# Joining the loads of a two-round decode kernel: 88 transfers for 101

## The chip, the core and the metric

The kernel runs on one core of a Trainium2 chip. A core has a matrix engine (PE, whose weight loads are listed as PEld), a vector engine (DVE), an activation engine (ACT), GpSimd (POOL), and a sequencer, SP, that here issues nearly all transfers from the chip's memory (HBM) to the on-chip SBUF. Sixteen DMA engines carry the transfers. The metric is the device time of one execution in microseconds (us); lower is better.

## What is computed

One decoding step for four sequences, `x` of 4 rows with 640 columns, in float32. A layer A (attention) and a layer B (an MLP) are applied alternately, twice, and both times with the same weights and the same caches:

```python
x = x + A(layernorm(x), k_cache, v_cache, wq, wo)
x = x + B(layernorm(x), w1, w2)
x = x + A(layernorm(x), k_cache, v_cache, wq, wo)
x = x + B(layernorm(x), w1, w2)
# A: 32 heads of 128; q = x @ wq; softmax(q k^T / sqrt(128)) v over the last 1024 cached positions; then @ wo
# B: relu(x @ w1) @ w2, with 1728 hidden columns
```

All of it rests on data that is used once in a round: 32 heads with their share of `wq`, 1024 keys and values for each of four sequences, and their share of `wo`, and then `w1` and `w2`.

## The kernel before

The host packs each head's data into one record of 9,472 float32 columns on 128 partitions (`REC`): 640 columns of `wq` (0 to `K`), 4,096 of keys (`K` to `V`), 4,096 of values (`V` to `WO`), and 640 of `wo`. A record is 4.85 MB. The 32 records lie one behind the other in HBM, so one transfer can span several records, or end inside one. `w1` and `w2` stand in a second array, `wm`.

SBUF holds five records at a time in a tile `store` (`NS = 5`), and beside it a tile `ring` of 4,832 columns and two tiles `kept` and `kept2` for parts that stay.

The kernel goes through two rounds. The first takes records 0 to 31 and then the MLP. The second begins with records 27 to 31, which are still in `store`, then takes 0 to 26, and then the MLP. For each record, PE computes the query (`query`, line 388), the scores of the keys (`scores`, 401), the weighted sum of the values (`values`, 438) and the product with `wo` (`project`, 457). The loop is skewed: in the step of record n, PE does the scores of n+1, the values of n, the query of n+2, and the projection of n, in this order. Every engine's instructions are in the order in which they are written.

Transfers are planned as a list, `items`, of source columns and a place in SBUF. The list is filled by small helpers: `piece` (207) loads columns of one record, `group` (211) loads several records in fewer transfers that are cut inside records, `ending` (217) orders the last three records of a round, and `weight` (197) loads columns of `wm`. `pump` (285) issues items in the order of the list, on SP's queue, and stops at the first one whose place still holds data in use. `done` (307) marks columns as used up after the instruction that reads them last, and calls `pump`. So a transfer is issued when the last column of its place has been read, and all later ones wait behind it.

`home(h, r)` (180) gives the place of record h: five places in turn. In the first round of the kernel before, record 0 comes in two transfers, records 1 to 4 in three (`FOUR`), record 5 in two, 6 to 9 in three, and 10 to 24 in three for each five (`FIVE`). The cut points of `FOUR` and `FIVE` lie inside records, so that the next transfer can start before the whole record has been read. Record 5 (`SIXTH`) keeps its last 2,176 columns in `kept2` for the second round, and record 26 its last 2,176 in `kept`.

At the change of rounds, record 0 is loaded into `ring` and into a free part of one place (`IN_RING`), while the MLP of the first round still empties `ring`; then the rest of record 0 and records 1 to 5 flow into the pieces of the five places as records 27 to 31 give them up. This is the list `places` (line 257), whose cuts fall where the engines' reads begin. After that, records have whole places again: 6, 7 and 8 one transfer each, 9 to 13 and 14 to 18 as `FIVE`, 19 to 23 as `LAST_FIVE`, and the last three by `ending`. The second MLP's weights go into two places of `store`.

The input `x` comes by four small transfers on ACT's queue at the start; PE's first matrix product waits for it. A wrapper class (line 94) issues all instructions, so most rows of the profile carry its line, L105 (L102 for the first of an engine); rows are told apart by their tiles. `misc<-xT,store` is a query, `sc_ps<-store,qT` scores, `o_ps<-store,scratch` values, `acc<-store,oTs` a projection, `sc_ps<-store,xT` the MLP's first product and `acc<-store,scratch` its second.

Of the kernel before, what the change touches and what calls it, by code (L numbers as in the profile page):

```python
# [32 lines left out]
F32 = mybir.dt.float32  # L33
# [5 lines left out]
P = 128  # L39
B, D, H, DH, W, FF = 4, 640, 32, 128, 1024, 1728  # L40
NB = 4
FD = D // NB
# [4 lines left out]
WQ, K, V, WO = 0, D, D + 4 * W, D + 8 * W  # L47
REC = 2 * D + 8 * W
HALF = REC // 2
VH = 2 * W  # L50

NS = 5
# [5 lines left out]
TCOLS = len(TILES) * FD  # L58
RING = 4832
KEPT = WO - 3 * 512  # L60
SIXTH = 5
KEPT2 = WO - 3 * 512
PARKED = 2048
FROM = V - 512
W2 = KB * FF
# [6 lines left out]
            (W2 + 2560, W2 + 4480, "spare", 0), (W2 + 4480, W2 + 6080, "ring", 0), (W2 + 6080, W2 + 7840, "ring", 1600),  # L72
            (W2 + 7840, WM, "ring", 3456)]

IN_RING = [(640, 1152, "ring", 4256), (1152, 3200, "spare", 0), (3200, 4736, "ring", 0), (4736, 6272, "ring", 1536),
           (6272, 7296, "ring", 3072), (8832, 8992, "ring", 4096)]
IN_SLOT = [(0, K), (7296, WO), (8992, REC)]

CUTS = [*range(0, K, DH), *range(K, WO, 512), *range(WO, REC + 1, FD)]
W1_SLOT = [[0, 1], [2], [3], [4]]  # L80
W2_SLOT = [22, 20, 8, 4]
LATE = 6

# [29 lines left out]
def decode_kernel(ctx: ExitStack, tc: tile.TileContext, xf, rec, wm, out):  # L113
    nc = tc.nc
    pe, dve, act, pool, sp = (InOrder(tc, e) for e in (nc.tensor, nc.vector, nc.scalar, nc.gpsimd, nc.sync))
    sb = ctx.enter_context(tc.tile_pool(name="sb", bufs=1))
# [72 lines left out]
    buffers = {"store": store, "ring": ring, "kept": kept, "kept2": kept2}  # L189

    def load(src, lo, hi, buf, col, parts):
        items.append((src[:, lo:hi], buf, col, hi - lo, parts))

    def place(buf, col):
        return ("store", spare * REC + FROM + col) if buf == "spare" else (buf, col)

    def weight(r, lo, hi, buf, col):
        buf, col = place(buf, col)
        load(wm, lo, hi, buf, col, [(("w", r), lo, hi, col)])


    def run(r, lo, hi, buf, col):
        parts = [(("rec", r, h), max(lo - h * REC, 0), min(hi - h * REC, REC), col + max(h * REC - lo, 0))
                 for h in range(lo // REC, (hi - 1) // REC + 1)]
        load(rec, lo, hi, buf, col, parts)

    def piece(r, h, lo, hi, buf="store", col=None):
        run(r, h * REC + lo, h * REC + hi, buf, home(h, r) * REC + lo if col is None else col)


    def group(r, h, sizes):
        lo = 0
        for size in sizes:
            run(r, h * REC + lo, h * REC + lo + size, "store", home(h, r) * REC + lo)
            lo += size

    def ending(r, hs, late):
        a, b, c = hs[-3:]
        end = WO if late else REC
        last = WO if late else KEPT  # L220
        for h, lo, hi in ((a, 0, V), (b, 0, V), (a, V, end), (c, 0, V), (b, V, end), (c, V, V + VH), (c, V + VH, last)):
            piece(r, h, lo, hi)
        if late:
            for h in hs[-1:] + hs[-LATE:-1]:
                if h == LAST - 1:
                    piece(r, h, WO, REC, "kept", WO - KEPT)
                else:
                    piece(r, h, WO, REC)


    hs = order[0]
    piece(0, hs[0], 0, V)
    piece(0, hs[0], V, REC)
    group(0, 1, FOUR)
    for h in hs[5:-3]:
        if h in GROUPS[0]:
            group(0, h, GROUPS[0][h])
        if any(g <= h < g + sum(z) // REC for g, z in GROUPS[0].items()):
            continue
        piece(0, h, 0, KEPT if h == LAST - 1 else KEPT2 if h == SIXTH else WO if h >= H - LATE else REC)  # L240
        if h == SIXTH:
            piece(0, h, KEPT2, REC, "kept2", 0)
# [18 lines left out]
    stream = [(new[0], lo, hi) for lo, hi in IN_SLOT] + [(h, 0, KEPT2 if h == SIXTH else REC) for h in new[1:6]]  # L261
    for buf, lo, hi in places:
        while stream:
            h, c, end = stream[0]
            cut = max(x for x in [*CUTS, end] if x <= min(end, c + hi - lo))
            if cut <= c:
                break
            piece(1, h, c, cut, buf, lo)
            lo += cut - c
            stream[:1] = [(h, cut, end)] if cut < end else []  # L270
    assert not stream
    for h in new[6:-3]:
        if h in GROUPS[1]:
            group(1, h, GROUPS[1][h])
        if not any(g <= h < g + sum(z) // REC for g, z in GROUPS[1].items()):
            piece(1, h, 0, REC)
    ending(1, hs, False)
    for ks in W1_SLOT:
        weight(1, ks[0] * FF, (ks[-1] + 1) * FF, "store", home(LAST + 1, 0) * REC + ks[0] * FF)
    n = 0  # L280
    for size in W2_SLOT:
        weight(1, W2 + n * FD, W2 + (n + size) * FD, "store", home(LAST + 2, 0) * REC + n * FD)
        n += size

    def pump():

        while items:
            src, buf, col, n, parts = items[0]
            if any(b == buf and x < col + n and col < y for b, x, y in live):
                return  # L290
            sp.dma_start(buffers[buf][:, col:col + n], src)
            live.append((buf, col, col + n))
            for key, lo, hi, c in parts:
                at.setdefault(key, []).append((lo, hi, buf, c))
            items.pop(0)
# [19 lines left out]
    def free(buf, a, b):  # L315
        if a < b:
            rest = []
            for bb, u, v in live:
                if bb != buf or v <= a or b <= u:
                    rest.append((bb, u, v))  # L320
                else:
                    rest += [(bb, p, q) for p, q in ((u, a), (b, v)) if p < q]
            live[:] = rest


    def park(i):
        a = spare * REC + FROM
        to, lo, hi = ((misc, 0, 512), (sc_ps[1], 512, 1536), (o_ps, 1536, 2048))[i]
        act.copy(to, store[:, a + lo:a + hi])
        free("store", a + lo, a + hi)  # L330
        pump()

    def unpark(i):
        b = home(LAST, 0) * REC
        a = b + (K, K + 512, K + VH, K + VH + 512)[i]
        copy = dve.tensor_copy if i in (1, 2) else act.copy
        copy(store[:, a:a + 512], (sc_ps[1][:, :512], sc_ps[1][:, 512:], o_ps, misc)[i])
        live.append(("store", a, a + 512))
        if i == 2:
            dve.memset(o_ps, 0.0)  # L340
        if i == 3:
            c = spare * REC
# [160 lines left out]
    for r in range(2):  # L503
        hs = order[r]
# [8 lines left out]
        if r:  # L513
            unpark(2)
            unpark(3)
        weights(0, ((0, 1), (1, 2)))
        for n, h in enumerate(hs[:-2]):
            i = n - (H - late)
# [3 lines left out]
            end = n == H - 3  # L522
# [17 lines left out]
        if not r:  # L540
            park(0)
# [5 lines left out]
        if not r:  # L547
            park(1)
        output_T(late - 2)
        if not r:  # L550
            park(2)
# [50 lines left out]
```

## Time and profile before

| | |
|---|---|
| three runs | 712.23, 712.61, 714.89 us; median 712.61 |
| the profiled execution | 711.53 us, its span 709.7 us |
| mean granted PE clock | 0.819 |
| busy: PE, DVE, ACT | 71%, 45%, 14% of the span |
| record and weight transfers (SP's queue q1) | 14,544 packets, 301.69 MB |
| mean rate over the span | 426 GB/s |

The span runs from the first to the last instruction; the time of a run holds a little more. Busy digits are tenths of a slice, of which the span has 40. A packet is what one DMA engine moves at a time: a transfer to 128 partitions has one for each partition's row of columns, eight on each engine, and one small packet for each engine that reports its end: 144 in all, and 101 transfers make 14,544. In the list of DMA issues, the last number is the time from issue to landing, which includes all the work that stands in the queue ahead.

### The profile page before, as it was taken

The page shows a single profiled execution, that of the slowest core. Times are in us where ns is not written, and L with a number is a line of the kernel's source. Part 1 is how long each engine was busy: PE and PEld are TensorE (multiplying, and loading weights), DVE is VectorE, ACT ScalarE, POOL GpSimd, SP SyncE. Part 2 cuts the span into 40 slices and gives each one's busy share as a digit, 9 for nine tenths or more (in the row PEclk, how much of TensorE's full clock was granted, in tenths as well). Part 3 has the DMA queues.
Part 4 walks back from the last instruction along what each step waited for, and adds up shares of the span by engine and source line. Part 5 has one row for each costly group of instructions (what it writes and reads, how often), then busy time and mean ns, then how long its engine had stood idle before and what let it go on. Part 6 is the DMA issues. An engine that isn't in the chain of part 4 may idle for free.

```text
span 709.7 us, 8716 instructions
## 1 busy us (share of the span) xinstructions
PE 503.7 (71%) x3722; PEld 203.4 (29%) x3722; DVE 317.4 (45%) x647; ACT 101.4 (14%) x216; POOL 1.1 (0%) x9
## 2 busy tenths in 40 slices
PE   4388386478566578879878898675577686776885
PEld 2123132232232223333313333231222231233322
DVE  3244253253443453545641866634244252453661
ACT  0111010011010110111120321201011011011120
POOL 0000000000000000000000000000000000000000
PEclk9987787577787776877999999968677676897899
DMA  9999999999999999999999999999999999999997
GB/s 400 421 453 408 454 410 459 417 439 441 428 433 426 424 451 420 424 425 430 427 408 408 417 435 422 448 425 453 428 428 437 439 432 430 432 427 419 427 425 303
DMA packets 14614, 302.24 MB, mean 426 GB/s; under 512 B 1632, under 2 KB 2032, under 8 KB 6256
## 3 DMA queue, kind: packets, MB, share of 16 engines
q1 hardware_dynamic: 14544, 301.69, 99.2%
q8 instruction: 29, 0.48, 0.2%
q14 instruction: 9, 0.07, 0.0%
q10 hardware_dynamic: 32, 0.01, 0.0%
HBM read 301.61 MB, written 0.08 MB: 425 GB/s over the span
## 4 chain that ended last, share of the span: by engine, by line
DMA 73%; PE 21%; DVE 3%; issue 1%; ACT 1%; another core or an unknown queue 0%; SPq 0%; ACTq 0%; DVEq 0%
DMA store<-rec 67%; PE o_ps L105 8%; PE sc_ps L105 7%; DMA store<-wm 3%; DMA ring<-wm 3%; PE misc L105 3%; PE acc L105 3%; DVE scratch L105 1%; DVE o_ps L105 1%; ACT oTs L105 1%; DVE small L105 0%; DVE store L105 0%; PE t_ps L105 0%; SPq L105 0%
## 5 line engine op out<-in xcount | busy, mean ns | idle before, releaser
L105 PE MATMUL sc_ps<-store,qT 128*4 128x512 f32 x1014 | 190.6, 837 | 24.4 <-DMA store<-rec 22.4
L105 PE MATMUL misc<-xT,store 128*128 128x4 f32 x620 | 97.2, 283 | 121.4 <-DMA store<-rec 121.1
L105 PE MATMUL o_ps<-store,scratch 128*16 128x512 f32 x954 | 143.8, 680 | 2.2 <-DMA store<-rec 1.2
L105 PEld LDWEIGHTS misc<-xT,store 128*128 128x128 f32 x620 | 91.8, 230 | 178.5 <-DMA store<-rec 145.7
L105 DVE TENSOR_REDUCE small<-sc_ps 128x1 f32<-128x1024 f32 x64 | 78.3, 1224 | 139.9 <-PE sc_ps L105 139.9
L105 ACT ACTIVATE sc_ps<-sc_ps,small 128x1024 f32<-128x1024 f32 (+1 forms) x68 | 71.1, 1046 | 319.6 <-DVE small L105 318.3
L105 DVE STREAM_TRANSPOSE sc_ps<-sc_ps 128x1024 f32<-128x1024 f32 (+1 forms) x70 | 81.7, 1167 | 0.1
L105 DVE TENSOR_TENSOR qT<-misc,rows 128x4 f32<-128x4 f32 x61 | 9.5, 155 | 135.6 <-PE misc L105 135.6
L105 DVE TENSOR_TENSOR o_ps<-o_ps,of_block 128x512 f32<-128x512 f32 x62 | 43.3, 699 | 52.3 <-PE o_ps L105 50.9
L105 PEld LDWEIGHTS o_ps<-store,scratch 128*16 128x16 f32 x954 | 33.3, 114 | 114.4 <-issue 101.1
L105 PEld LDWEIGHTS sc_ps<-store,qT 128*4 128x4 f32 x1014 | 32.5, 106 | 107.8 <-issue 65.4
L105 PE MATMUL acc<-store,oTs 128*4 128x160 f32 x478 | 34.3, 368 | 17.2 <-ACT oTs L105 16.4
L105 DVE TENSOR_REDUCE scratch<-o_ps 128x128 f32<-128x512 f32 x62 | 42.9, 691 | 2.1
L105 ACT COPY oTs<-o_ps 128x4 f32<-128x4 f32 x62 | 10.1, 162 | 226.6 <-PE o_ps L105 226.6
L105 PE MATMUL o_ps<-rows,scratch 128*128 128x4 f32 x124 | 27.0, 288 | 13.2 <-DVE scratch L105 13.0
L105 PEld LDWEIGHTS o_ps<-rows,scratch 128*128 128x128 f32 x124 | 22.8, 229 | 20.8 <-DVE scratch L105 17.7
L105 DVE TENSOR_TENSOR scratch<-sc_ps,mrt 128x128 f32<-128x128 f32 (+1 forms) x70 | 19.6, 280 | 2.7
L105 DVE TENSOR_SCALAR mrt<-of_batch,small 128x4 f32<-128x4 f32 x64 | 14.7, 229 | 2.2
L105 PE MATMUL acc<-kept,small 128*1 128x344 f32 (+1 forms) x44 | 14.7, 445 | 0.0
L105 PEld LDWEIGHTS acc<-store,oTs 128*4 128x4 f32 x478 | 6.6, 84 | 23.2 <-ACT oTs L105 21.2
L105 DVE STREAM_TRANSPOSE scratch<-small 128x32 f32<-128x32 f32 x64 | 12.8, 201 | 0.8 <-ACT sc_ps L105 0.8
L105 ACT ACTIVATION_READ_ACCUMULATOR sc_ps<-sc_ps,small 128x1 f32 x64 | 12.3, 193 | 0.0
(86 smaller groups left out, 118.1 us busy)
## 6 DMA issues: line engine op xcount, KB each, us to landing
store<-rec SPq DMA_DIRECT2D x10, 7872.0 KB, 28.9
store<-rec SPq DMA_DIRECT2D x5, 7936.0 KB, 33.4
store<-rec SPq DMA_DIRECT2D x14, 2368.0 KB, 27.3
store<-rec SPq DMA_DIRECT2D x6, 4736.0 KB, 26.7
store<-rec SPq DMA_DIRECT2D x4, 6336.0 KB, 27.7
store<-rec SPq DMA_DIRECT2D x2, 7104.0 KB, 29.7
store<-rec SPq DMA_DIRECT2D x2, 6272.0 KB, 43.6
store<-rec SPq DMA_DIRECT2D x2, 4416.0 KB
```

The source lines that it names most:

```text
L105: r = build(*args, **kwargs)
```

## The change

The first 2,176 columns of record 0 (the query weights and three blocks of keys; `FIRST = K + 3 * 512`) get a place of their own in front of the five places, and `store` grows by as much. `kept2` goes. Record 0 is loaded in the first round at column 0 of `store`, records 0 to 4 lie one behind the other from there, and all later records use the five places shifted by `FIRST`. So the first columns of record 0 are still there in the second round, and only columns 2,176 onward are loaded again. Record 5 is loaded whole in the second round.

Transfers are joined:

- in the first round, records 0 to 24 come five at a time in three transfers, from the very first record on;
- at the end of a round, the first of the last three records comes in one transfer and not two;
- at the change of rounds, record 0 takes four transfers and one for its `wo`, and records 1 to 5 flow as one stream whose transfers may cross from one record to the next (14 transfers); one place piece now spans two neighbouring places;
- in the second round, records 6 to 8 come in two transfers (`THREE`);
- two of the four `w1` pieces of the second MLP are joined.

The instructions of the computing engines stay as they are, apart from the columns that they read.

```diff
-SIXTH = 5
-KEPT2 = WO - 3 * 512
+FIRST = K + 3 * 512
...
-IN_RING = [(640, 1152, "ring", 4256), (1152, 3200, "spare", 0), (3200, 4736, "ring", 0), (4736, 6272, "ring", 1536),
-           (6272, 7296, "ring", 3072), (8832, 8992, "ring", 4096)]
-IN_SLOT = [(0, K), (7296, WO), (8992, REC)]
+IN_RING = [(2176, 2688, "ring", 4256), (2688, 4736, "spare", 0), (4736, 6272, "ring", 0), (6272, 8832, "ring", 1536)]
...
-W1_SLOT = [[0, 1], [2], [3], [4]]
+W1_SLOT = [[0, 1], [2, 3], [4]]
...
-FOUR = [REC + 3200, REC + 3072, 2 * REC - 6272]
 FIVE = [REC + 6272, 2 * REC - 3072, 2 * REC - 3200]
 LAST_FIVE = [REC + 4736, 2 * REC - 4736, REC, REC]
-GROUPS = [{6: FOUR, 10: FIVE, 15: FIVE, 20: FIVE}, {9: FIVE, 14: FIVE, 19: LAST_FIVE}]
+THREE = [REC + HALF, REC + HALF]
+GROUPS = [{h: FIVE for h in range(0, 25, 5)}, {6: THREE, 9: FIVE, 14: FIVE, 19: LAST_FIVE}]
...
-    store = sb.tile([P, NS * REC], F32, name="store")
+    store = sb.tile([P, FIRST + NS * REC], F32, name="store")
...
-    kept2 = sb.tile([P, REC - KEPT2], F32, name="kept2")
...
     def home(h, r):
 
-        return h % NS if not r or h >= LAST else (h - 6 + LAST) % NS
+        if r:
+            return FIRST + (h if h >= LAST else h - 6 + LAST) % NS * REC
+        return (0 if h < NS else FIRST) + h % NS * REC
...
-    at = {("rec", 1, LAST - 1): [(KEPT, REC, "kept", 0)], ("rec", 1, SIXTH): [(KEPT2, REC, "kept2", 0)]}
+    at = {("rec", 1, LAST - 1): [(KEPT, REC, "kept", 0)], ("rec", 1, 0): [(0, FIRST, "store", 0)]}
...
-        for h, lo, hi in ((a, 0, V), (b, 0, V), (a, V, end), (c, 0, V), (b, V, end), (c, V, V + VH), (c, V + VH, last)):
+        for h, lo, hi in ((a, 0, end), (b, 0, V), (c, 0, V), (b, V, end), (c, V, V + VH), (c, V + VH, last)):
...
-    piece(0, hs[0], 0, V)
-    piece(0, hs[0], V, REC)
-    group(0, 1, FOUR)
-    for h in hs[5:-3]:
+    for h in hs[:-3]:
         if h in GROUPS[0]:
             group(0, h, GROUPS[0][h])
...
-    places = [("store", old[i] * REC + lo, old[i] * REC + hi) for i, lo, hi in (
-        (0, 0, K), (0, K + 1024, K + VH), (0, K + VH + 1024, V), (1, 0, K + VH), (1, K + VH, V), (0, V, WO), (0, WO, REC),
-        (2, 0, V), (1, V, REC), (3, 0, V), (2, V, REC), (4, 0, FROM), (3, V, REC),
-        (4, FROM + PARKED, REC), (4, FROM, FROM + PARKED))] + [("ring", 0, RING)]
+    places = [("store", old[i] + lo, old[j] + hi) for i, lo, j, hi in (
+        (0, 0, 0, K), (0, K + 1024, 0, K + VH), (0, K + VH + 1024, 0, V), (1, 0, 1, K + VH), (1, K + VH, 1, V),
+        (0, V, 0, WO), (0, WO, 0, REC), (2, 0, 2, V), (1, V, 1, REC), (3, 0, 3, V), (2, V, 2, REC), (3, V, 4, FROM),
+        (4, FROM + PARKED, 4, REC), (4, FROM, 4, FROM + PARKED))] + [("ring", 0, RING)]
...
+    cuts = [h * REC + x for h in new[1:6] for x in CUTS]
+    c, end = new[1] * REC, new[6] * REC
     for buf, lo, hi in places:
...
+        if lo == old[0] + WO:
+            piece(1, new[0], WO, REC, buf, lo)
+        elif c < end:
+            cut = max(x for x in cuts if x <= min(end, c + hi - lo))
+            run(1, c, cut, buf, lo)
+            c = cut
```

More of the change, by code (lines that the diff above doesn't have):

```diff
@@ L180, in home @@
     def home(h, r):
-        return h % NS if not r or h >= LAST else (h - 6 + LAST) % NS
+        if r:
+            return FIRST + (h if h >= LAST else h - 6 + LAST) % NS * REC
+        return (0 if h < NS else FIRST) + h % NS * REC
     items = []
-    at = {("rec", 1, LAST - 1): [(KEPT, REC, "kept", 0)], ("rec", 1, SIXTH): [(KEPT2, REC, "kept2", 0)]}
+    at = {("rec", 1, LAST - 1): [(KEPT, REC, "kept", 0)], ("rec", 1, 0): [(0, FIRST, "store", 0)]}
     live = []
     spare = home(H - 1, 0)
-    buffers = {"store": store, "ring": ring, "kept": kept, "kept2": kept2}
+    buffers = {"store": store, "ring": ring, "kept": kept}
     def load(src, lo, hi, buf, col, parts):
@@ L194, in place @@
     def place(buf, col):
-        return ("store", spare * REC + FROM + col) if buf == "spare" else (buf, col)
+        return ("store", spare + FROM + col) if buf == "spare" else (buf, col)
     def weight(r, lo, hi, buf, col):
@@ L207, in piece @@
     def piece(r, h, lo, hi, buf="store", col=None):
-        run(r, h * REC + lo, h * REC + hi, buf, home(h, r) * REC + lo if col is None else col)
+        run(r, h * REC + lo, h * REC + hi, buf, home(h, r) + lo if col is None else col)
     def group(r, h, sizes):
@@ L213, in group @@
         for size in sizes:
-            run(r, h * REC + lo, h * REC + lo + size, "store", home(h, r) * REC + lo)
+            run(r, h * REC + lo, h * REC + lo + size, "store", home(h, r) + lo)
             lo += size
@@ L231, in decode_kernel @@
     hs = order[0]
-    piece(0, hs[0], 0, V)
-    piece(0, hs[0], V, REC)
-    group(0, 1, FOUR)
-    for h in hs[5:-3]:
+    for h in hs[:-3]:
         if h in GROUPS[0]:
             group(0, h, GROUPS[0][h])
[L238 to L242, printed above, removed]
+        if h >= 25:
+            piece(0, h, 0, KEPT if h == LAST - 1 else WO if h >= H - LATE else REC)
         if h == LAST - 1:
@@ L256, in decode_kernel @@
         piece(1, new[0], lo, hi, *place(buf, col))
-    places = [("store", old[i] * REC + lo, old[i] * REC + hi) for i, lo, hi in (
-        (0, 0, K), (0, K + 1024, K + VH), (0, K + VH + 1024, V), (1, 0, K + VH), (1, K + VH, V), (0, V, WO), (0, WO, REC),
-        (2, 0, V), (1, V, REC), (3, 0, V), (2, V, REC), (4, 0, FROM), (3, V, REC),
-        (4, FROM + PARKED, REC), (4, FROM, FROM + PARKED))] + [("ring", 0, RING)]
-    stream = [(new[0], lo, hi) for lo, hi in IN_SLOT] + [(h, 0, KEPT2 if h == SIXTH else REC) for h in new[1:6]]
-    for buf, lo, hi in places:
[L263 to L271, printed above, removed]
+    places = [("store", old[i] + lo, old[j] + hi) for i, lo, j, hi in (
[4 more added lines that the diff above has]
+    c, end = new[1] * REC, new[6] * REC
+    for buf, lo, hi in places:
+        if lo == old[0] + WO:
[4 more added lines that the diff above has]
+            c = cut
+    assert c == end
     for h in new[6:-3]:
@@ L278, in decode_kernel @@
     for ks in W1_SLOT:
-        weight(1, ks[0] * FF, (ks[-1] + 1) * FF, "store", home(LAST + 1, 0) * REC + ks[0] * FF)
+        weight(1, ks[0] * FF, (ks[-1] + 1) * FF, "store", home(LAST + 1, 0) + ks[0] * FF)
     n = 0
     for size in W2_SLOT:
-        weight(1, W2 + n * FD, W2 + (n + size) * FD, "store", home(LAST + 2, 0) * REC + n * FD)
+        weight(1, W2 + n * FD, W2 + (n + size) * FD, "store", home(LAST + 2, 0) + n * FD)
         n += size
@@ L326, in park @@
     def park(i):
-        a = spare * REC + FROM
+        a = spare + FROM
         to, lo, hi = ((misc, 0, 512), (sc_ps[1], 512, 1536), (o_ps, 1536, 2048))[i]
@@ L333, in unpark @@
     def unpark(i):
-        b = home(LAST, 0) * REC
+        b = home(LAST, 0)
         a = b + (K, K + 512, K + VH, K + VH + 512)[i]
@@ L341, in unpark @@
         if i == 3:
-            c = spare * REC
+            c = spare
             at["rec", 1, H - 1] = [(0, FROM, "store", c), (FROM, V, "store", a), (V, V + 1024, "store", b + K),
```

## The prediction

> **What bounds the kernel now.** I read the page first: busy shares, DMA queues, the chain that ended last and the DMA issues.
>
> ```profile
> span 709.7 us, 8716 instructions
> PE 503.7 (71%) x3722; PEld 203.4 (29%) x3722; DVE 317.4 (45%) x647; ACT 101.4 (14%) x216; POOL 1.1 (0%) x9
> DMA  9999999999999999999999999999999999999997
> q1 hardware_dynamic: 14544, 301.69, 99.2%
> DMA 73%; PE 21%; DVE 3%; issue 1%; ACT 1%; another core or an unknown queue 0%; SPq 0%; ACTq 0%; DVEq 0%
> store<-rec SPq DMA_DIRECT2D x10, 7872.0 KB, 28.9
> out<-scratch SPq DMA_DIRECT2D x1, 80.0 KB, 1.6
> ```
>
> The transfers that SP issues keep the 16 DMA engines at 99.2% of the span; no slice but the last is below 9. PE is busy 71%, but mostly waits for data and catches up. So the time is bytes over rate, plus what each transfer adds, plus a head and a tail. A wait of PE counts only if it lets the DMA queue run empty.
>
> Next the DMA view by stretch, first of long loads, then of mixed ones, then of short ones around the change of rounds:
>
> ```profile
> DMA packets 433, 24.23 MB, mean 433 GB/s; under 512 B 47, under 2 KB 47, under 8 KB 47
> ...
> DMA packets 1960, 25.59 MB, mean 427 GB/s; under 512 B 220, under 2 KB 220, under 8 KB 768
> ...
> DMA packets 1955, 8.07 MB, mean 404 GB/s; under 512 B 219, under 2 KB 475, under 8 KB 1664
> ```
>
> These are 134 to 190, 300 to 360 and 380 to 400 us. Each transfer leaves 16 packets under 512 B (one an engine), so the three stretches hold about 3, 14 and 14 transfers.
>
> **The change: the term that counts.** The bytes do not change: the second round skips 2,176 columns of the first record, where it skipped 2,176 columns of the sixth, and the SBUF reserved is the same. PE, DVE and ACT do the same work on the same shapes. So what goes is 13 transfers of 101: 5 in round one's records, 5 at the change of rounds, 2 in round two's records, 1 in the weights.
>
> Price of one: at 433 GB/s the 8.07 MB of the third stretch take 18.64 us; they took 20, so 1.36 us for 13.7 transfers, 0.10 us each. The 25.59 MB of the second take 59.10; they took 60, so 0.90 over 13.75, 0.065 each. I take the middle, 0.08, since the 13 lie in both kinds of stretch: 13 x 0.08 = 1.05 us. Ends: 0 (the skipped overheads may be refilled by skew between engines) and 13 x 0.10 = 1.4. SP also issues 13 times 0.33 us less, hidden, since SP mostly waits.
>
> [...]
>
> **What hides the joins.** A joined load is issued when the last of its places is free, so later. It costs nothing while the queue still has work. I call margin: time from issue to landing, less the load's own time at 433 GB/s, less 1.4 us of latency (the 80 KB store lands after 1.6 and moves for 0.2).
>
> (a) The first five records. Three loads of 7.9 MB replace five. The DMA view from 1.6 to 2 us has the first packets (there are none before 1.6), and then comes PE's start (columns: start, duration, work, idle before):
>
> ```profile
> DMA packets 9, 0.17 MB, mean 426 GB/s; under 512 B 0, under 2 KB 0, under 8 KB 0
> ...
> 9.64 0.87 PE L102 MATMUL acc<-scratch,ring 128*128 128x160 f32 x2 [9.64 <-DMA scratch<-xf]
> 11.79 2.29 PE L105 MATMUL misc<-xT,store 128*128 128x4 f32 x10 [0.27 <-DVE xT L105]
> 16.67 1.89 PE L105 MATMUL sc_ps<-store,qT 128*4 128x512 f32 x8
> 29.43 2.29 PE L105 MATMUL misc<-xT,store 128*128 128x4 f32 x10 [10.87 <-DMA store<-rec]
> 35.35 2.42 PE L105 MATMUL o_ps<-store,scratch 128*16 128x512 f32 x16
> ...
> q10 hardware_dynamic: 32, 0.01, 0.9%
> ...
> store<-rec SPq DMA_DIRECT2D x1, 2368.0 KB, 8.2
> ...
> 9.01 0.33 SPq L105 DMA_DIRECT2D store<-rec  x1
> ...
> store<-rec SPq DMA_DIRECT2D x1, 6336.0 KB, 51.6
> ```
>
> The first load (issued at 0.8) landed at 9.0, the fifth record at 9.01 + 51.6 = 60.6. The input x, on ACT's queue (q10), came at 9.64, just behind the first load: its 32 small packets all went between 4.5 and 9.2 us, taking turns with that load's rows. Now the first load is 8.06 MB, 18.6 us instead of 5.6, and rows are 3.3 times as long. x then comes some 0.6 x 3.3 = 2 us behind a landing at about 21.5: 23.5 (ends 21.5 and 1.8 + 7.8 x 3.3 = 27.6). PE starts 14 us later. From x to the end of the first scores takes 8.9 (9.64 to 18.56), the next query to the first values 8.3 (29.43 to 37.77), one more record 8.8 (504.02 to 512.81, rows below): the place of the next load is free at 23.5 + 26.0 = 49.5. The three loads end at about 60.4, so it had to be issued by 59. Margin 9.5 us: the late start is hidden.
>
> The second load of the next group needs more than in the old alignment, as the places sit 2,176 columns further on: values of the fourth record, not only the output of the third. That step in the trace (a load landing, 146.84 + 25.4 = 172.2, and PE after it):
>
> ```profile
> 146.84 0.33 SPq L105 DMA_DIRECT2D store<-rec  x1
> ...
> store<-rec SPq DMA_DIRECT2D x1, 7872.0 KB, 25.4
> ...
> 179.58 0.33 SPq L105 DMA_DIRECT2D store<-rec  x1
> ...
> 182.31 2.34 PE L105 MATMUL o_ps<-store,scratch 128*16 128x512 f32 x16
> ```
>
> Output after 7.3, first half of values after 182.31 + 1.2 - 172.2 = 11.3. So issue at 60.4 + 11.3 = 71.7, needed by 60.4 + 18.6 - 1.4 = 77.6: margin 5.9. The load issued at 146.84 lives with 25.4 - 18.6 - 1.4 = 5.4, and the queue stays full.
>
> (b) The change of rounds. The tightest issue:
>
> ```profile
> 394.33 0.33 SPq L105 DMA_DIRECT2D store<-rec  x1
> ...
> store<-rec SPq DMA_DIRECT2D x1, 1344.0 KB, 6.4
> ```
>
> Own time 3.2, so margin 6.4 - 3.2 - 1.4 = 1.8. Ahead of it the first record's rest is 160 columns (0.2 us) shorter, the next pieces 32 columns longer (0.04), and three transfers fewer stand there (0.25): 1.4 us left, tight but positive. The place is freed by a resident record's scores, which wait for no new load. The last ring load now waits for the MLP's last tiles, about 0.4 us later, under that same queue.
>
> (c) The sixth to eighth new record of round two come in two loads, and the group after them needs the fifth's values:
>
> ```profile
> 457.17 0.33 SPq L105 DMA_DIRECT2D store<-rec  x1
> ...
> store<-rec SPq DMA_DIRECT2D x1, 7872.0 KB, 46.8
> ...
> 504.02 2.29 PE L105 MATMUL misc<-xT,store 128*128 128x4 f32 x10 [11.34 <-DMA store<-rec]
> 510.92 1.89 PE L105 MATMUL o_ps<-store,scratch 128*16 128x512 f32 x16
> ```
>
> Landed at 504.0, so the loads before it end at 485.4 and the first of the two joined ones 16.8 earlier, at 468.6. PE then needs 8.1 (504.02 to the first half of values at 512.1): issue at 476.7 instead of 457.2, needed by 484. Margin 7.3.
>
> (d) The tail. Record 24 (first of the last three) lands whole, one 2.4 MB load (5.6 us) later:
>
> ```profile
> 646.61 0.33 SPq L105 DMA_DIRECT2D store<-rec  x1
> ...
> store<-rec SPq DMA_DIRECT2D x1, 2368.0 KB, 35.9
> ...
> 663.09 1.28 PE L105 MATMUL misc<-xT,store 128*128 128x4 f32 x10
> ...
> 695.99 0.91 PE L105 MATMUL sc_ps<-store,xT 128*4 128x432 f32 x8 [0.69 <-DMA store<-wm]
> 700.26 1.80 PE L105 MATMUL acc<-store,scratch 128*4 128x160 f32 x44 [2.38 <-DMA store<-wm]
> 703.96 1.27 PE L105 MATMUL acc<-store,scratch 128*4 128x160 f32 x32 [1.90 <-DMA store<-wm]
> ...
> 706.30 0.11 PEld L105 LDWEIGHTS acc<-store,scratch 128*4 128x4 f32 x8 [0.34 <-DMA store<-wm]
> ```
>
> The last of five such loads landed at 682.5, so the second at 682.5 - 3 x 5.6 = 665.7; less 1 us saved by then, 664.7. The query at 663.09 becomes 1.7 us late. PE's waits for weights at 695.99, 700.26 and 703.96 (0.7, 2.4, 1.9 us) absorb it even though the weights come 1 us sooner. The joined weight pieces land where the second did. No price.
>
> Sum: the profiled execution took 711.53 us (span 709.7); 711.53 - 1.05 = 710.5. The median of the three runs, 712.61, stands 1.1 above it; I forecast on the median: 712.61 - 1.05 = **711.5 us**.
>
> **Rivals.**
> 1. *x comes much later (slower).* If x's four small loads each wait for a whole load of SP's queue, x comes with the third load, at 60.4; the place for the fourth is free at 60.4 + 26.0 = 86.4, and the queue stands empty from 60.4 to 87.8: 712.6 + 27.4 - 1 = 739. Against it: 32 packets within 4.5 to 9.2 us, during one load. It costs from x at 33 on, and decides (over 0.5%) from 38. 3 in 100. [...]
> 2. *The turn runs dry (slower).* If the joined places come free a scores step (1.9 us) later at each of four joins, 7.6 us stand against the 1.4 of margin: 712.6 - 1 + 6.2 = 718. For it: the smallest margin. Against: the steps that free them are in the same order. Decides from 6 us late. 6 in 100.
> 3. *More gain (faster).* 301.69 MB at 433 GB/s is 696.7; with the 1.8 before the first packet and 3.4 after the last (706.30 to the span's end), 702. All transfers together lose 7.6; were all of that in the 13, 705. 4 in 100.
> 4. *Each transfer's latency is not hidden (faster):* 13 x 1.4 = 18, so 694. The DMA row of nines speaks against it; 3 in 100.
>
> **How the numbers follow.** The forecast has 84 in 100. Its range takes the term's ends (0 to 1.4) and the spread of the runs (711.5 to 714.9, the profiled one among them): 709.7 to 714.0. That leaves out the rivals, 16 in 100. A change within 0.5% (3.6 us, about what a measurement of this kernel can tell from none) is the forecast alone: faster 0.07, same 0.84, slower 0.09.
>
> **What would show it.** Right: q1 packets 14544 - 13 x 144 = 12,672 with 301.69 MB, DMA share still 99%, PE's first matmul at 22 to 28 us, an issue of a 7.9 MB load near 50 us, 404 GB/s risen around the turn. Wrong: any slice but the last under 9 in the DMA row, above all near 60, 79, 395 or 485 us; or a tail after the last load longer than 3.5 us.

## The result, and the profile after

| | before | after |
|---|---|---|
| median of the runs (22 each, on one chip) | 712.88 us | 715.06 us |
| lowest to highest | 711.47 to 714.89 | 712.60 to 717.20 |
| the profiled execution, its span | 711.53 us, 709.7 us | 715.46 us, 713.7 us |

The ratio after to before is 1.0027, with a 95% interval of 1.0018 to 1.0037: the change costs some 2 us. That is within the 0.5% which the prediction called no change, but it has the wrong sign, its interval excludes 1, and 715.06 us lies above the predicted range of 709.7 to 714.0. The ratios in this text are those on record for the runs, and not quotients of the two medians that stand beside them.

The page of the changed kernel, in the rows that answer to those shown of before (DMA share by slice, GB/s by slice, the queue of records and weights, and the chain that ended last):

```profile
DMA  9999999999999999999999999999999999999997
GB/s 396 448 404 449 441 415 441 444 419 435 440 431 424 447 427 424 416 447 421 423 382 376 381 435 427 454 430 436 440 422 435 440 426 430 440 422 430 427 425 293
...
q1 hardware_dynamic: 12672, 301.68, 98.8%
...
DMA 28%; PE 16%; DVE 4%; issue 1%; ACT 1%; DVEq 0%; ACTq 0%
```

The packets are the 12,672 that 88 transfers should leave, 144 each (in the trace of the changed kernel the store of the output, alone in its stretch from 710 us on, left 128 packets of 512 B to 2 KB and 16 under 512 B), and the bytes are the same. The row of nines hides the loss: a 9 is anything from 90% up, and the slices are 17.8 us long. The GB/s row below it shows it. Slices 21 to 23, from 357 to 410 us, move 382, 376 and 381 GB/s, and no other slice between the first and the last is that low.

The same stretch by windows (columns: window; length, then busy time and count of PE, PEld, DVE, ACT and POOL; granted PE clock; DMA share; GB/s), before:

```profile
360.00:400.00 40.00, 31.21 (x336) 12.44 (x328) 14.35 (x45) 9.10 (x18) 0.00 (x0) 1.00 1.02 407
364.00:372.00 8.00, 4.96 (x43) 1.40 (x41) 1.61 (x8) 1.19 (x2) 0.00 (x0) 1.00 1.01 403
...
380.00:400.00 20.00, 16.95 (x186) 7.96 (x184) 10.40 (x32) 5.53 (x10) 0.00 (x0) 1.00 1.02 404
```

and after:

```profile
360.00:400.00 40.00, 32.75 (x326) 12.30 (x330) 15.50 (x49) 10.36 (x20) 0.00 (x0) 0.92 0.96 369
364.00:372.00 8.00, 7.40 (x90) 2.91 (x82) 4.02 (x13) 3.31 (x6) 0.00 (x0) 1.00 0.89 340
...
380.00:400.00 20.00, 17.81 (x188) 7.75 (x184) 7.72 (x26) 4.32 (x8) 0.00 (x0) 0.84 0.96 353
```

In these 40 us the rate falls by 38 GB/s, so 1.52 MB less is moved. At the full queue's 433 GB/s (before, 134 to 190 us) that is 3.5 us, most of the 4.0 us by which the profiled spans differ. Two places hold it: 364 to 372 us (63 GB/s, 0.50 MB), in the first MLP, and 380 to 400 us (51 GB/s, 1.02 MB), at the change of rounds. The prediction had said that the second would rise.

What was late there? The chain of waits of before, in order of time (start, duration, what), runs through this stretch in transfers:

```profile
327.44 31.96 DMA store<-rec
...
369.34 6.76 DMA ring<-wm
```

The chain of after runs there through PE and DVE, and begins only at 361 us; what came before is not resolved (hence the 28% DMA on its page):

```profile
364.36 0.70 DVE scratch L102
...
365.49 0.93 PE acc L102 x24
...
371.02 6.71 DMA ring<-wm
```

So PE and DVE arrive late at the end of the first round. Where they fell behind is seen one record earlier. PE's timeline there, before (start, duration, work, count, idle before):

```profile
334.77 1.28 PE L105 MATMUL misc<-xT,store 128*128 128x4 f32 x10
...
336.77 1.90 PE L105 MATMUL sc_ps<-store,qT 128*4 128x512 f32 x16
...
349.70 1.28 PE L105 MATMUL misc<-xT,store 128*128 128x4 f32 x10 [1.12 <-DMA store<-rec]
...
354.65 1.91 PE L105 MATMUL o_ps<-store,scratch 128*16 128x512 f32 x16 [1.20 <-DMA store<-rec]
...
359.53 1.05 PE L105 MATMUL sc_ps<-store,scratch 128*16 128x512 f32 x8 [1.03 <-DMA store<-rec]
```

and after, with the windows of PE's clock around it:

```profile
338.62 2.11 PE L102 MATMUL misc<-xT,store 128*128 128x4 f32 x10 [4.82 <-DMA store<-rec]
...
341.08 3.60 PE L102 MATMUL sc_ps<-store,qT 128*4 128x512 f32 x16
...
335.40:338.80 3.40, 0.18 (x2) 0.19 (x2) 0.00 (x0) 0.00 (x0) 0.00 (x0) 1.00 0.99 420
338.90:342.30 3.40, 3.40 (x19) 2.42 (x23) 1.47 (x5) 0.16 (x1) 0.00 (x0) 0.50 1.01 435
342.40:345.70 3.30, 3.30 (x20) 0.66 (x16) 1.52 (x3) 0.00 (x0) 0.00 (x0) 0.50 1.00 431
```

This is the query of record 29, the first of the last three records of round one. In the kernel before its keys came ahead of its values, in a transfer of their own; now it is one load, and the query waits 4.82 us for all of it. The query comes 3.85 us later than before. From 335.4 to 338.8 us PE was busy for 0.18 us, the beginning of the query itself; after that the granted clock was 0.50 for two stretches of 3.4 us, and the same 16 scores matmuls took 3.60 us for 1.90. Before, three waits for records follow, of 1.12, 1.20 and 1.03 us; after, PE waits for no record any more until the end of the round, so all three are used up, and the rest of the delay stays. At the end of the round ACT copies the last columns out of the place that the MLP's weights go to, and the next transfer of SP's queue waits for that copy. Before:

```profile
361.13 0.59 ACT L105 COPY o_ps<-store 128x512 f32<-128x512 f32 x1
...
361.74 0.33 SPq L105 DMA_DIRECT2D store<-wm  x1
```

After:

```profile
365.72 0.59 ACT L102 COPY o_ps<-store 128x512 f32<-128x512 f32 x1
...
366.34 0.33 SPq L102 DMA_DIRECT2D store<-wm  x1
```

The copy and the issue are 4.6 us late, all later weights wait behind it, and the queue runs low at 364 to 372 us (340 GB/s for 403).

At 380 to 400 us, where the prediction had found the smallest margin of all (1.8 us), the places come free late too. This is the same delay, handed on by the weights. PE itself had nearly caught up: it starts on the fourth transfer of the MLP's weights at 372.17 us, before at 371.99. But the weights that were issued late also land late. The wait for the sixth transfer, before and then after:

```profile
376.14 0.53 PE L105 MATMUL sc_ps<-ring,xT 128*4 128x432 f32 x1 [0.58 <-DMA ring<-wm]
```

```profile
377.77 0.53 PE L102 MATMUL sc_ps<-ring,xT 128*4 128x432 f32 x1 [2.05 <-DMA ring<-wm]
```

Behind this wait the granted clock is 0.56 from 379.4 to 382.8 us (before, 1.00 in the 3.4 us behind the same wait), and PE's first query of round two comes at 390.35 us for 387.20, 3.1 us late.

All of this is read from one pair of traces. It doesn't show that the join causes it, nor how much of the loss comes from the late landing and how much from the halved clock. That is what the experiments are for.

### The profile page after: what moved, and what is told of

Read it like the earlier page. It is cut to its first block, busy times and chain, and to the rows that moved or that the text cites. A ratio compares the mean times of both kernels' runs of the same rounds, so it can differ in the third digit from the quotient of the medians.

```text
span 713.7 us, 8687 instructions
## 1 busy us (share of the span) xinstructions
PE 498.1 (70%) x3722; PEld 203.1 (28%) x3722; DVE 317.7 (45%) x647; ACT 101.3 (14%) x216; POOL 1.1 (0%) x9
## 3 DMA queue, kind: packets, MB, share of 16 engines
q1 hardware_dynamic: 12672, 301.68, 98.8%
## 4 chain that ended last, share of the span: by engine, by line
DMA 28%; PE 16%; DVE 4%; issue 1%; ACT 1%; DVEq 0%; ACTq 0%
DMA store<-rec 26%; PE sc_ps L102 6%; PE o_ps L102 5%; PE acc L102 3%; DMA ring<-wm 2%; PE misc L102 2%; DVE scratch L102 1%; DVE o_ps L102 1%; DVE small L102 0%; ACT oTs L102 0%; DVE sc_ps L102 0%; PE t_ps L102 0%; ACT sc_ps L102 0%; DVE store L102 0%; DVE mrt L102 0%
## 5 line engine op out<-in xcount | busy, mean ns | idle before, releaser
L102 PE MATMUL sc_ps<-store,qT 128*4 128x512 f32 x1022 | 182.9, 807 | 41.9 <-DMA store<-rec 40.0
L102 PE MATMUL o_ps<-store,scratch 128*16 128x512 f32 x956 | 149.3, 695 | 1.5 <-DVE scratch L102 1.2
L102 PE MATMUL acc<-store,oTs 128*4 128x160 f32 x488 | 32.7, 350 | 17.0 <-ACT oTs L102 17.0
```

The lines of the kernel that those rows point to most:

```text
L102: r = build(*args, **kwargs)
```

## The experiments

The theory (A): the join of record 29 in round one makes PE late, and the 12 other removed transfers are about neutral. Rivals: the loss comes from the new list of places at the change of rounds (B); or it is the join in the tail, record 24 (C); within A, it is the halved clock rather than the late landing that costs.

### Splitting record 29 again

The changed kernel, with the first of the last three records split again in round one only (89 transfers):

```diff
-        for h, lo, hi in ((a, 0, end), (b, 0, V), (c, 0, V), (b, V, end), (c, V, V + VH), (c, V + VH, last)):
+        first = ((a, 0, V), (b, 0, V), (a, V, end)) if late else ((a, 0, end), (b, 0, V))
+        for h, lo, hi in (*first, (c, 0, V), (b, V, end), (c, V, V + VH), (c, V + VH, last)):
```

> The changed kernel, but record 29 at the end of the first round comes again in two loads (query weights and keys, then values, with record 30's keys between); all other joins stay. Theory A (the join of record 29 makes the query of 29 wait for a whole record, PE ends the round some 4.6 us later, the copies that free the spare place come later, and the transfer queue runs empty in the first MLP): the query of 29 no longer waits for 338.6, the first load into the spare place is issued near 361.7 and not 366.3, the DMA share from 370 to 400 us is back at 1.00, and the time is about 1 us below the kernel before, 711.9 us. Theory B (the joined loads at the change of rounds themselves run the queue dry): the time stays near the changed kernel's, 715, and the DMA share from 380 to 400 us stays near 0.96.

Measured: 713.41 us beside 712.61 of before on the same chip, ratio 1.0007 (0.9993 to 1.0021); 711.9 had been expected. The transfer into `store` is issued at 362.60 us, the rate from 364 to 372 us is back at 399 GB/s, and most of the loss is gone. But at the change of rounds the trace shows what had been named as the sign of theory B, a DMA share of 0.96:

```profile
380.00:400.00 20.00, 17.33 (x180) 7.55 (x177) 9.13 (x26) 5.36 (x10) 0.00 (x0) 0.91 0.96 373
...
396.00:398.00 2.00, 2.00 (x20) 0.34 (x12) 1.90 (x5) 0.00 (x0) 0.00 (x0) 0.70 0.60 133
```

The kernel split in both rounds, below, has the same instructions up to the tail of round two, and its trace has 1.00 and 395 GB/s from 380 to 400 us. So this stretch differs by some 20 GB/s between executions of the same work, and the share there doesn't decide between A and B; the times have to.

### That join alone, in the kernel before

The kernel before, with only this one join made, in round one (100 transfers):

```diff
-        for h, lo, hi in ((a, 0, V), (b, 0, V), (a, V, end), (c, 0, V), (b, V, end), (c, V, V + VH), (c, V + VH, last)):
+        first = ((a, 0, end), (b, 0, V)) if late else ((a, 0, V), (b, 0, V), (a, V, end))
+        for h, lo, hi in (*first, (c, 0, V), (b, V, end), (c, V, V + VH), (c, V + VH, last)):
```

> The kernel before, with this one join alone: record 29 at the end of the first round in one load, 100 transfers. Theory A: 2 to 4 us slower than the kernel before, some 715 to 716.5 us, with the first load into the spare place near 366 us. Theory B: no change, 712.8 us.

Measured: 714.93 us beside 712.61, ratio 1.0029 (1.0009 to 1.0048), as much as the whole change. Its profiled execution was the slowest of its runs (span 718.6 us, runs 712.32 to 720.37), so its trace shows the mechanism at its worst. The issue, the clock behind the query, the 40 us as above, and the worst of them:

```profile
365.87 0.33 SPq L105 DMA_DIRECT2D store<-wm  x1
...
340.00:346.00 6.00, 6.00 (x39) 2.18 (x38) 3.28 (x7) 0.16 (x1) 0.00 (x0) 0.62 0.99 423
...
360.00:400.00 40.00, 33.07 (x302) 13.07 (x302) 10.94 (x34) 8.12 (x17) 0.00 (x0) 0.82 0.94 353
...
396.00:404.00 8.00, 7.65 (x36) 3.27 (x36) 5.07 (x16) 4.33 (x8) 0.00 (x0) 0.50 0.49 154
```

From 396 to 404 us PE is busy 7.65 of 8 us at half clock, and the DMA engines have work for half the time. As far as the intervals tell, one removed transfer does all that the 13 together did. The new list of places isn't in this kernel, so B is not needed.

### Keeping PE's clock up while it waits

The changed kernel, with 8 products that go to spare columns between the values of record 27 and the query of record 29, in round one. The load of record 29 stays joined:

```diff
             values(r, h)
+            if not r and h == H - 5:
+                for _ in range(8):
+                    busy()
```

> The changed kernel, with 8 filler products on PE (about 5 us of work on data that is there, into columns that nothing reads) between the values of record 27 and the query of 29 in the first round, where PE waits 4.8 us for the joined load. In the changed kernel PE's granted clock then fell to 0.53 (340 to 346 us) and its products took twice as long. Theory A1 (the slow PE after the wait makes up the larger part of the lateness): the clock stays near 1.0, the spare place comes free about 2.5 us sooner, and the time is half way back, 713 to 714 us. Theory A2 (the late landing alone is the cause): no change, 715 us.

Measured: 713.68 us beside 712.61, ratio 1.0009 (0.9995 to 1.0022). By its time alone this kernel is told apart neither from before nor from the changed kernel; its trace says more. The query comes at the same moment as in the changed kernel, but at full clock:

```profile
333.62 4.79 PE L102 MATMUL acc<-kept,small 128*1 128x344 f32 x16
338.62 1.28 PE L102 MATMUL misc<-xT,store 128*128 128x4 f32 x10 [0.22 <-DMA store<-rec]
...
358.03 1.05 PE L102 MATMUL o_ps<-store,scratch 128*16 128x512 f32 x8 [0.62 <-DVE scratch L102]
...
360.11 2.15 PE L102 MATMUL sc_ps<-store,scratch 128*16 128x512 f32 x16 [0.46 <-DVE scratch L102]
...
363.77 0.33 SPq L102 DMA_DIRECT2D store<-wm  x1
...
340.00:346.00 6.00, 5.37 (x46) 2.13 (x45) 4.79 (x11) 1.37 (x3) 0.00 (x0) 1.00 1.01 429
...
360.00:400.00 40.00, 33.05 (x342) 13.21 (x342) 15.97 (x46) 10.12 (x19) 0.00 (x0) 0.96 1.01 403
```

The issue comes at 363.77 and not 366.34: of the 4.6 us, 2.6 were the halved clock and 2.0 the landing. With 2.0 us the queue stays full: 403 GB/s where before had 407 and the changed kernel 369, and PE's first query of round two comes at 387.23 us, before at 387.20. So in this trace the late landing alone lies within what the queue covers, and the clock pushes it past that.

In the rows of the changed kernel the two stretches at 0.50 stand right behind one with 0.18 us of work in it. PE was busy for 3.40 and 3.30 us of them, and from 345.8 to 349.2 us the clock was 1.00 again. With the fillers it was 1.00 in the same four stretches, from 335.4 to 349 us. How long PE has to wait before the clock falls was not measured.

### Splitting the first of the last three in both rounds

The changed kernel with the loop in `ending` as in the kernel before (90 transfers):

```diff
-        for h, lo, hi in ((a, 0, end), (b, 0, V), (c, 0, V), (b, V, end), (c, V, V + VH), (c, V + VH, last)):
+        for h, lo, hi in ((a, 0, V), (b, 0, V), (a, V, end), (c, 0, V), (b, V, end), (c, V, V + VH), (c, V + VH, last)):
```

> The changed kernel, with the first of the last three records in two loads at the end of both rounds. Theory A: the same as with the first round's alone, 711.9 us within 0.3, since the tail of the second round ends with a wait for the last weights. Theory C (the join at the end of the second round also costs, through a later end of PE's chain): 1 to 2 us faster than that kernel.

Measured: 712.74 us beside 712.61, ratio 0.9996 (0.9982 to 1.0009); 711.9 within 0.3 had been expected. No loss is left, with 11 of the 13 transfers still removed and the new list of places in use. That settles A against B. Of C, the join in the tail, the times say little: this kernel and the one split in round one only (1.0007) differ by less than their intervals.

One thing differs from before at the change of rounds. Before, and then this kernel:

```profile
396.00:398.00 2.00, 2.00 (x18) 0.28 (x10) 1.92 (x4) 0.00 (x0) 0.00 (x0) 1.00 1.00 407
```

```profile
394.00:396.00 2.00, 2.00 (x12) 0.30 (x8) 1.86 (x7) 0.54 (x2) 0.00 (x0) 0.50 1.08 395
396.00:398.00 2.00, 2.00 (x20) 0.44 (x12) 1.85 (x3) 0.02 (x1) 0.00 (x0) 0.78 0.83 292
```

A small hole (292 GB/s for 407, so 0.23 MB, 0.5 us) follows a stretch of half clock. Does the clock cause it?

### Fillers at the start of round two, in two kernels

The same fillers at the start of round two, one in front of the first scores' wait and one behind the second; once on the kernel with both splits, once on the kernel before:

```diff
         query(r, hs[1], 1)
         if r:
+            busy(256, t_ps, 2)
             unpark(2)
...
             scores(r, hs[n + 1], s)
+            if r and n == 0:
+                busy(256, t_ps, 2)
```

> The changed kernel with the first of the last three records in two loads in both rounds, and two short filler products on PE at the start of the second round, in its two waits for VectorE (392.3 to 393.2 and 395.1 to 395.9 us in the profile of the same kernel without them). There the granted clock fell to 0.50 (394 to 396 us), the next place came free 0.5 us later than in the kernel before, and the DMA share fell to 0.83 (396 to 398 us). Theory D (this half clock, not the joined loads, eats the gain of the missing transfers): the clock stays 1.0 there, the DMA share stays 1.0, and the time is 711.7 us, about 1 below the kernel before. Theory E (a missing transfer saves next to nothing): no change from that kernel, 712.6.

> The kernel before with the same two fillers. Its profile had the clock at 1.0 there. Theory D: its slower runs are runs in which the clock halves at this place, so the median falls by some tenths, to 712.2, and the spread of the runs (711.6 to 715.5) becomes smaller. Otherwise no change, 712.6.

Measured, on another chip than the kernels above: 713.56 us, ratio 0.9991 (0.9974 to 1.0009), and 712.30 us, ratio 0.9986 (0.9966 to 1.0005), both beside 713.05 of before. Neither is told apart from no change, and the spread of the runs with fillers (711.78 to 715.50 on the kernel before) isn't clearly smaller. In the first of them the clock stays up and the hole remains:

```profile
396.00:398.00 2.00, 1.75 (x16) 0.26 (x16) 1.93 (x4) 0.00 (x0) 0.00 (x0) 1.00 0.84 309
```

So for this hole the clock isn't the cause, and that part of the theory fell; the 711.7 us expected for this kernel weren't reached either. Nor is it peculiar to the new places: the kernel before with the fillers moves 347 GB/s in the same 2 us. It is worth about 0.5 us here, and 1.3 us in the kernel split in round one only (133 GB/s, shown above). What makes it is open.

### The price of one transfer

The kernel before, with each of the 25 loads that `group` makes (23 span several records, two are one record) cut in three at the marks inside the records (50 transfers more, 151 in all, no join anywhere):

```diff
         for size in sizes:
-            run(r, h * REC + lo, h * REC + lo + size, "store", home(h, r) * REC + lo)
-            lo += size
+            ends = [max(x for x in marks if x <= lo + size * k // 3) for k in (1, 2)] + [lo + size]
+            for to in ends:
+                run(r, h * REC + lo, h * REC + to, "store", home(h, r) * REC + lo)
+                lo = to
```

> The kernel before with each of the 25 transfers that span several records cut in three: 151 transfers, the same bytes in the same order. It measures the price of a transfer where the queue is full. By the price of the prediction, 0.08 us each: 50 x 0.08 = 4 us slower, 716.6. By theory E: within 0.5 of the kernel before.

Measured: 716.04 us beside 713.05, ratio 1.0033 (1.0011 to 1.0054). 0.0033 of 713.05 us is 2.35 us; over 50 transfers that is 0.047 us each (0.016 to 0.077 by the interval). The traces agree. From 80 to 280 us, before and then this kernel:

```profile
DMA packets 1616, 86.81 MB, mean 434 GB/s; under 512 B 176, under 2 KB 176, under 8 KB 176
```

```profile
DMA packets 4809, 86.18 MB, mean 431 GB/s; under 512 B 535, under 2 KB 535, under 8 KB 535
```

The packets under 512 B, 16 a transfer, show 22 more transfers in these 200 us. They cost 0.63 MB, 1.45 us at 433 GB/s, 0.066 us each. A part of a load can also be issued before the whole could, so this is the price net of that.

### All joins, with the clock kept up at both places

The changed kernel with all 88 transfers, the 8 fillers in round one and the fillers at the start of round two:

```diff
             values(r, h)
+            if not r and h == H - 5:
+                for _ in range(8):
+                    busy()
...
         if r:
+            busy(256, t_ps, 2)
...
+            if r and n == 0:
+                busy(256, t_ps, 2)
```

> The changed kernel as it is, 88 transfers, with both sets of fillers: the 8 before the query of record 29 and the two at the start of the second round. Theory A1 with D (PE's halved clock after its waits carries the loss, not the later landing): no slower than the kernel before, 712 to 712.6 us. If the later landing itself counts: 713.5 or more.

Measured: 713.07 us beside 713.05 of before, ratio 0.9994 (0.9975 to 1.0013):

```profile
340.00:346.00 6.00, 5.66 (x48) 2.48 (x47) 4.40 (x9) 1.37 (x3) 0.00 (x0) 1.00 0.99 420
...
360.00:400.00 40.00, 33.17 (x352) 13.16 (x352) 16.64 (x50) 10.12 (x19) 0.00 (x0) 1.00 1.01 400
```

The join of record 29 is in place, and the loss isn't there: the interval lies below that of the changed kernel (1.0018 to 1.0037), which was measured beside before in another set of runs. The time lies between the two that had been expected (up to 712.6, or 713.5 and more). None of the kernels is told apart from before as a faster one.

This trace also says something of C, the join in the tail. Record 24's query waits for its load, and from there to the end the chain runs through PE and no transfer:

```profile
665.90 1.28 PE L102 MATMUL misc<-xT,store 128*128 128x4 f32 x10 [1.36 <-DMA store<-rec]
...
704.06 3.99 PE L102 MATMUL acc<-store,scratch 128*4 128x160 f32 x112
```

The granted clock is 0.64 from 668 to 681 us; before, it was 1.00 from 664 to 677 us, behind the same query at 663.09. PE comes to the second MLP at 698.83 us for 691.78, 7 us late, where its waits for weights had been 5.0 us in all. The last packet of weights has gone by 706.1 us, much as before (706.0), but PE's last product ends at 708.05 us, before at 706.75. From packet to product that is 1.9 us for 0.7, so in this execution the join in the tail cost about 1.2 us. Wherever the tail is joined in the new kernel (the changed kernel, split in round one only, and the two with fillers at record 29), the query waits (1.4 to 4.0 us) and the chain holds no transfer behind that load; where it is split (before, and split in both rounds) the query doesn't wait and the chain runs through the weights' transfers. But in all of these others it is 0.7 to 0.8 us from packet to product, so how much of the times C makes up stays open.

## Why the prediction was wrong

**The bound** held at this place: bytes over rate, and a wait of PE counts only if the queue runs empty. That is how the 2 us came about (369 GB/s for 407 from 360 to 400 us); with the same join and the clock kept up, at 400 and 403 GB/s, no loss was told apart.

**The sums** hold some slips. 13 x 0.10 is 1.3 and not 1.4, and 13 x 0.08 is 1.04. From the ends that are named (a term of 0 to 1.4, runs of 711.5 to 714.9) the range would be 710.1 to 714.9, not 709.7 to 714.0; 715.06 lies above both.

**The opening, (a), and the group after records 6 to 8, (c)** came out nearly as worked out. PE's first product and the issues, after:

```profile
22.07 0.87 PE L99 MATMUL acc<-scratch,ring 128*128 128x160 f32 x2 [22.07 <-DMA scratch<-xf]
...
49.69 0.33 SPq L102 DMA_DIRECT2D store<-rec  x1
...
72.76 0.33 SPq L102 DMA_DIRECT2D store<-rec  x1
...
480.27 0.33 SPq L102 DMA_DIRECT2D store<-rec  x1
```

The prediction had 23.5, 49.5, 71.7 and 476.7. The last is 480.3 because all of round two comes about 4 us later. No slice near 60, 79 or 485 us shows a dry queue. So the first rival (x much later) is out. The third and the fourth (705 and 694 us) are out as well: no kernel with fewer transfers came near.

**The step that failed is the list of what hides the joins, (a) to (d).** The change joins the first of the last three records at the end of *a* round, so in both rounds. The prediction counted both among its 13 transfers, but walked only the one in the tail of round two, record 24 in (d), where it gave "No price". Record 29, at the end of round one, was never followed to its query. The two places differ in what comes behind them. In the tail the weights are issued in time in spite of the delay (the last of them between 685 and 686 us both before and in the run with the clock kept up), and PE has waits to absorb it. In round one the weights and then the next round's records stand behind the delay, in places that PE must first give up. By the method of (d): the keys of record 31 landed at 349.70 us, two loads of 5.6 us earlier is 338.5, and the query that had run at 334.77 would have come some 3.8 us late. The three waits of before at 349.70, 354.65 and 359.53 would have taken 3.35 of that. The 0.5 us left lie within the 1.4 of (b), so the step would have read "no price" here too. The run with the clock kept up bears this out in kind, not in size: it was 2.0 us late, since PE then came to wait for DVE (0.62 and 0.46 us, rows above), and there was no loss in the queue. The walk alone would have shown where to look, not that it costs.

**The margin of (b), 1.4 us, assumed that PE's chain at the change of rounds stays where it was.** "The place is freed by a resident record's scores, which wait for no new load" is true, but these scores stand behind the first MLP, and that behind record 29 and the weights that wait for it. PE began round two 3.1 us late against a margin of 1.4. So the second rival (the turn runs dry, 6 in 100) named one of the two right places, but another mechanism: not only the joined places there come free late, but all of PE's work arrives late, and in the kernel with record 29's join alone, which has the old places, the turn runs drier still (154 GB/s from 396 to 404 us).

**What turned a late landing into a loss** was a cost that no term of the prediction had: behind PE's idle time of 4.82 us the granted clock was 0.50 for 6.7 us, so that some 3.4 us of work at full clock was lost (6.7 x 0.50, an estimate). With the 3.85 us by which the query was late that is 7.2 us, against 3.35 us of waits that could absorb it; 3.9 would be left by this estimate, and 4.6 were seen. Of these, 2.6 go away with the fillers. A wait that PE could nearly have caught up with became one that it couldn't.

**The gain was over-sized.** By its sum, 1.05 us was to be saved, 0.08 a transfer. Measured directly, a transfer cost 0.047 us (0.016 to 0.077, in the kernel with 50 more), so 13 are worth 0.6 us; the price taken is just above the interval. The two stretches from which it was taken also held small rows (768 and 1,664 packets under 8 KB), and the division by transfers put whatever these cost on the transfers; that this is the reason was not tested. A gain of 0.6 us is 0.0009 of the time, which none of the intervals here (0.0010 to 0.0022 either way) tells from nothing.

**The tail, (d).** The last weights, after:

```profile
706.13 4.49 PE L102 MATMUL acc<-store,scratch 128*4 128x160 f32 x112
...
710.16 0.11 PEld L102 LDWEIGHTS acc<-store,scratch 128*4 128x4 f32 x8 [0.29 <-DMA store<-wm]
```

From the last wait for weights to the span's end is 3.5 us, where it was 3.4: no longer tail, as forecast. But the three waits of PE that were to absorb 1.7 us are gone; PE works through the second product with no wait ahead of it, and in this trace it had run at a clock of 0.51 from 669.9 to 676.8 us, behind record 24's query, which waited 2.33 us. So the cover was used up, and (d) left out the same cost as the walk of record 29 would have: the slow clock behind the wait. "No price" held in this trace only just; in the kernel with the clock kept up at the two other places, PE ended about 1.2 us after it could have. The times don't resolve it.

## What to carry to other kernels

When a change is made at "the end of a round" or "in the helper", list every place where the helper is called, and walk each to the next transfer that hangs on it; the same join cost 2 us where the next stage's loads stood behind it, and in the tail, where none did, no more than the times resolve (1.2 us in one trace). The waits of PE in the changed kernel of 4.82, 2.05 and 2.33 us had a slow stretch behind them (0.50 for 6.7 us, 0.56 for 3.4, 0.51 for 6.9); before, behind the 0.58 us at the place of the 2.05, the clock was 1.00. So look in the trace for such a stretch, price the wait by its length plus what the stretch adds, and compare that sum with the smallest margin downstream, not with the margin at the place itself. Where the idle time couldn't be avoided here, products into spare columns kept the clock up (1.00 for 0.53 from 340 to 346 us): with them 88 transfers took the time of 101 (713.07 and 713.05 us).

## What the runs showed of the hardware

Behind a wait of 4.82 us PE ran for two stretches of 3.4 us at a granted clock of 0.50, and these added 2.6 us to the 2.0 us of delay that the late landing makes by itself. This kernel, whose DMA engines were busy for 98.8% of the span, so lost 0.3% to one late load and the slow clock behind it, in 40 us of its 714.

In the full queue of this kernel, a transfer to 128 partitions cost 0.047 us more than its bytes (0.016 to 0.077, from 151 transfers against 101). By that price there is little to be had from fewer transfers here: all 88 that remain would hold about 4 us (88 x 0.047, an estimate).

Why the DMA share falls at 396 to 398 us, to 0.83 and 0.84 with the new places and both splits, with a full clock too, and to 0.90 with the old places and the fillers, stays open. So does the spread of the runs of one kernel (711.5 to 719.2 us for the kernel before on one chip); that it comes from where the half-clock pieces happen to fall was only argued, and the fillers at the start of round two didn't show it.
